# A written-out order of 1,900 steps: the same steps in another order

## The chip, the cores and the metric

The kernel runs on one core of a Trainium2 chip. The metric is the time of one execution in microseconds of device time, as the median of several runs.

## What is computed

A causal attention that lets every query see only its six best chunks of 32 keys, and a gated feed-forward network on its output. B, H, S, D are 4, 8, 768, 64; the network goes from 512 to 1536 and back, for 3072 tokens. The reference, cut:

```python
k_chunks = k.reshape(B, H, nc, chunk, D)
k_min, k_max = np.min(k_chunks, axis=3), np.max(k_chunks, axis=3)
ub = np.sum(np.maximum(q[:, :, :, None, :] * k_min[:, :, None, :, :],
                       q[:, :, :, None, :] * k_max[:, :, None, :, :]), axis=-1)
ub = np.where(causal, ub, -1000000000.0)
top_chunks = np.argsort(ub, axis=-1)[..., -top_k:]
scores = scale * np.matmul(q, k.transpose(0, 1, 3, 2))
scores = np.where(mask, scores, -1000000000.0)      # mask: chosen chunk and causal
attn = np.exp(scores - np.max(scores, axis=-1, keepdims=True))
attn = attn / (np.sum(attn, axis=-1, keepdims=True) + 1e-09)
...
x = np.ascontiguousarray(attn_out.transpose(0, 2, 1, 3)).reshape(B * S, H * D)
xn = x / np.sqrt(np.mean(x * x, axis=-1, keepdims=True) + 1e-06) * rms_g
g = xn @ w_gate
out = g * (1.0 / (1.0 + np.exp(-g))) * (xn @ w_val) @ w_out
```

## The kernel before, in words

**Tiles and stages.** The 32 heads go in 16 pairs, numbered 0 to 15; four pairs make one of the four batches. For each pair:

- `kload`, `qload` (line 500, on SP's queue; 192 KB each as two transfers of 96 KB) bring k and q; `v` (line 476, on POOL's queue) brings the values.
- `kT`, `qT` (line 520) turn three tiles of 128 at a time on TensorE; `kE`, `qE` (lines 290 and 294) copy the result out of PSUM, on ACT or on DVE.
- `kmx`, `kmn`, `dif` (lines 549, 551, 602) make the chunks' extremes; `relu` (lines 636 and 638, on ACT, DVE or POOL) the positive part of q; `ub` (lines 737 and 795) the bounds on TensorE; `ubE`, `up`, `ubm` bring them into place.
- `max`, `grd`, `sel` (lines 653 to 691) choose the chunks. The choice is laid beside k and q as further rows of the matrices `ke` and `qs`, so that a score of a chunk that is not chosen comes out very low. For the first three pairs it is turned on TensorE (`selT`, `selC`), later by a transposing transfer (`qX`, line 560). `kC`, `qC`, `qN` (line 294, mostly on POOL) cast k and q. The casts of a later pair write the same set of matrices (`set`, three of them) that an earlier pair's scores read.
- `sc` (line 882) computes scores of up to 512 columns, `exp` (line 899, on ACT) their exponentials, `mask` (line 905, on POOL) the causal edge, `av` (line 918) the products with v, `xb` (lines 938 and 939) the division.

A batch that is complete is normed in two halves (`sq`, `eps`, `root`, `xs`; then `tp` on TensorE and its eviction `tpE` for the first batch, a transposing transfer `xT` for the others). Each half of 384 tokens goes through the network: twelve times a `gate` (line 1051), `tanh`, `tg`, `val` (line 1072) and `hh`, then three output groups of three `po` steps each (line 1092), an eviction `poE` and a store `out`. The weights come in halves, wg and wv (line 440) and wo (line 445), from POOL's queue; the first six of the twelve gates read the first half of wg, the first six vals the first half of wv. `busy` (line 339) is a matmul of zeros, which keeps TensorE at work in the first microseconds.

So the network of one batch overlaps the attention of the next.

**The order.** Nothing decides at run time. Each step is added with its dependences to a list, and its place there is its number. A text, `PROGRAM`, names the steps in the order in which they are emitted: a letter for the engine (P TensorE, A ACT, D DVE, G POOL, S SP), the number, and behind the colon the slots of the buffers that the step opens (the eight PSUM banks among them). Each engine runs its words in order, and the order on each queue is that of the words as well:

```python
for word in program.split():
    n, _, slots = word[1:].partition(":")
    s = self.steps[int(n)]
    s.eng = engines[word[0]]
    new = [b for b in s.opens if b.slot is None]
    for b, x in zip(new, slots.split(",") if slots else (), strict=True):
        b.slot = int(x)
    out.append(s)
```

A step whose input is late holds back everything behind it on its engine. A buffer in the same slot must have been read by all its users before it is opened again.

Words that come up below: S227 is the load of pair 2's q, S541 of pair 6's k, S470 of pair 5's k; G115 and G183 load the v of pairs 0 and 1; G76 and G78 load the halves of wg, G77 and G79 those of wv; P1260, P1265 and so on in fives are the first gates, P1268 and P1288 two of the first vals; G415 and G486 are relus of pairs 4 and 5.

Of the kernel before, what the change touches and what calls it, by code (L numbers as in the profile page):

```python
# [28 lines left out]
    "S83:0 S88:1 S89 S82 D3 G0 D56 D55 D53 D54 D60 G63 A2 G65 P4:0 D59 P5:1 G66 P6:2 D58 P7:3 D57 G67 P8:4 S154:2 "  # L29
    "P9:5 G68 P86:6 S159:3 P10:7 G72 A87:0 P11:0 A69 D97:0 P92:1 D96:0 P12:2 G64 S335:4 G73 P84:3 D93:1 P90:4 A85 "  # L30
    "P13:5 P14:7 A91 P15:6 D95 P16:0 A99:0 P17:2 G101 D94 S222:5 P157:1 P155:5 D98 G62 A158:2 D103:3 P18:3 G61 "
    "P19:7 P20:4 S71 D156 P104:6,0 G102 D1 D52 D165:1 G168:1 P160:2 S330:6 A106:0 P162:3 D164:1 G74 A105 P21:1 "
    "A161:4 P107:7 A163 G167 P336:4 S70 D108:0 P338:5 A171:5 P22:0 G166 D109:2 P23:6 P24:1 A100 D110 S541:0 "
    "P172:2,3 A337:6 D112:0 A339 D111 P225:7 A173:0 D174 P113:0 G346:3 A226:1 S227:1 P175:6 A114 P223:1 D176:1 "
    "P25:4 P26:5 D177:3 P331:2 P333:3 D178 A224 G115:0 S404:2 P119:7 D332:2 A334 P147:6 A179:1 P135:4 D340:4 "
    "A148:0 G170 P128:5 P116:0 A136:1 D180 S399:3 P544:1 A117:2 D341:2 P150:3 P125:2 A545:0 P181:6 P141:4 A151:3 "
    "D232:5 A126:4 P138:0 G342 G236:2 P347:1,3 A120:5 D182 A129:6 G169 P228:2 A139:7 P230:7 S546:5 G183:1 D348:0 "
    "A349 P542:5 D229:5 A231 P350:6 D233:3 A142:8 P190:0 G345:0 P118:1 P121 A239:6 P144:3 P149:2 D351:2 P152 "
    "P184:7 G234 G235 A191:9 D352:6 P240:4,6 D543 A145:2 G238 D353 A185:5 P215:0 P122:5 G251:2 A241:0 D242 P143 "
    "A216:0 P146 P131:3 P243:7 A354 P405:4 A123:3 G237 D244:0 P209:6 P140 P137 A132:8 P218:0 D245:7 P193:7 A210:2 "  # L40
# [12 lines left out]
    "D423 A1281:1 D424 G1339:1 P1270:5 D1262:2 A1286:3 S426 D1282:4 P1275:2 A1271:5 D1346:3 P1263:3 A1276:6 S425 "
    "D1272:7 P1265:7 D1277:0 P1305:1 D1343:0 A1266:1 S559:0 P1288:5 D550 D1264:0 P1344:2 G557:3 P1315:0 D1287:5 "
    "A1345 S564:4 D1267:6 P439:3 A1316:2 P449:6 D1289:1 P445:2 P1300:7 A450:3 D1269:2 P1295:5 G427:0 A440:4 "
    "D481:2 A1301:3 P1283:6 A446:7 D1317:1 G79 A1296:5 P457:4 D1302:6 P560:3 A458:6 P436:2 G482 D1297:2 P1347:0 "
    "G81 A561:1 P562:7 D1348 P565:4 A563 D1284:3 P428:5 P463:3 A437:0 D1340:1 P432:0 G572:0 P487:7,6 A429:2 "
    "D570:3 A464:9 P1273:2 G451 A489:0 D488 A566:4 P1341:5 G485:0 P567:3 A1306:3 D1342 P459:6 A433:1 P490:7 "
    "D1274:4 G430 P1364:4 D569:2 G80 P466:5 P1349:0 A467:5 D491:0 P465 P442:2 D571 D568 P1399:5 A443:8 D1307:5 "
    "P460:7 P452 D575:2 A1400:4 P1278:3 A461:6 D1401:7 P577:2,1 A1350:3 D492:3 A1365:4 D493 G494 P453:7 P1308:5 "  # L60
    "A582:0 D578 A454:9 P1298:1 D1309:5 G455 P583:2 G484:2 D1299:6 P579:7 P462 D1366:5 P456 P1389:5 G434 D581:2 "
    "G483 D580:1 P468 P1392:1 D585 A1390:2 D584 D469:1 G573 P1310:4 D586:4 P1318:7 D592:5 D495 P1402:2 D1351:4 "
    "S496 P1374:6 D1279:7 D1391:3 P438:0 P1354:3 S497 D1393:8 P1303:5 D1403:9 A1355:0 P1367:1 A1375:2 D587 "
    "A1311:3 S700:3 D1319:10 P1290:2 G588 D1356:7 G498:1 P1379:7 D1312:1 A1291:0 P1293:3 D1368:11 A1380:3 G576:2 "
    "D1304:12 P524:4 P1325:1 D1292:5 A525:3 G574:0 D1294:13 P503:5 P444 D1381:6 P510:2 G526 P431 P447 P528:4 D593 "
    "A511:6 P1313:3 D589 A529:9 G594 P435 D1376:0 P703:7 S591 A504:5 P701:2 D1314:14 P1394:4 D595 D702:0 P537:6 "
    "P507:5 S590 P520:3 A538:0 D704 A1395:5 P1326 A521:8 D1396:3 P513:2 G522 S597 P1359:6 A514:2 P539:7 P441 "
    "P499:3 P1327 D448 A500:7 S596 A1360:2 P534:4 G501 P598:2 D1328:0 P1352:0 A535:1 G505 S682:1 A508:0 P516:3 "
    "P523 P506:1 D1353:15 P1384:4 A599:4 D1361:1 A517:8 P530 P536 P531:5 S705:5 D710:7 A1385:5 P512 P509 P665:0 "
    "A532:5 G714:2 P515 P678:2 P527 D1386:4 P672:3 A666:9 P518 P675:6 G558:3 D711:1 S841:2 P533 A673:1 P606:5 "  # L70
    "P502 P669:4 A679:6 P644:0 A676:0 D540 P661:3 G667 P1320:2 A607:2 G713 S823:0 D519 A662:3 P685:6 A670:8 "
    "P674:7 G663 P680 P623:5 D686:5 P657:3 P668 P683:1 G715:1 S687:6 A658:5 A645:7 P671 P1321 D684 A624:1 G646 "
    "D693:2 P648:4 G625 P651:6 S1329 P640:3 A649:6 P654:0 D692:0 P612:1 A641:9 P1322 A613:8 G642 P677 P706:5 "
    "D1323:1 G696:0 A655:0 P650:4 P842:3 S828:4 D707:3 A652:6 P647 P614:1 G712 P609:2 G600 P656 A843:4 P664 "
    "P626:0 P643 A610:7 P653 D681 G694 P633:5 S1324 P708:6 A634:8 P659 P615:3 P601 P826:2 A709 P611 P824:7 S846:3 "
    "D827:2 P602:5 G716:6 P630:6 A825 D660 P1369:2 A616:0 A603:3 D834:0 P1357:7 A631:1 S987:1 P608 A1370:2 P619:3 "
    "D833:6 P690:4 G604 A620:9 P636:5 P617 P635 G699:0 P688:6 D1371:5 A691:1 P605 P627:3 A689 P632 S982:5 D618 "
    "P844:2 G858:1 A628:6 P1362:4 D1358:16 A845 P629 A698:0 P831:6 D852:3 G621 P1382:1 A637:5 G854:1 P622 P638 "
    "P718:3,7 D639 G695 D1363:17 A1425:1,0 G697:0 P1377:2 A1426:1 D719:0 G717:2 P849:5 A1424:2 P720:0 D850:5 "
    "P1404:4 A1510:2,0 G835 D1378:18 P847:3 D721:0 A1405:2 P829:5 D832:1 A1511:1 P1330:2 D1427:3 D1406:7 G1428:4 "  # L80
    "A848 D722:1 P1407:6 A830 A723 D1429:2 P1387:4 D1433:0 P724:3 S1430:1 P1331 D1408:19 D1383:20 P1397:0 S1434 "
    "D1431:3 P1372:5 D1398:21 P1409:7 S1432 D1388:22 D1373:23 P1419:6 D726 S1105:0 D733:5 P1414:1 D734 D725 P1420 "
    "G735 D736 P1415 D851:7 S737 P1455:0 D727:0 D728 P1440:4 S738 A1456:1 D730 P1332 A729 D853 A839:0 S731 "
    "P1460:5 A1441:0 A1512:2 P1410 A1461:2 S732 A1333:2 P1445:3 D1462:7 D1442:6 P983:2 P1411 D1513:6 S969:2 "
    "A984:3 G1514:1 A1446:3 P789:5 P785:4 D1412:0 G856:1 P1421 A790:4 S1334 D1447:4 A786:7 G838:0 S1413 P792:2 "
    "D857:6 P760:7 A1422:1 P781:5 S1110:6 G855 P747:3 A793:2 P1450:4 D1457:5 A748:0 D1517:1 P753:6 A782:8 P1470:2 "
    "S964:3 A761:3 P739:0 D1519:2 P1435:3 A1471:2 G762 A740:1 D1472:0 P1108:5 S1123:4 A1436:3 P743:7 G783 P1438:0 "
    "D1109:4 A1451:1 D1437:2 A754:6 P1416 S1520 A744:9 P755:2 P1106:5 G745 D1417:2 P816:3 G741 P746 S1128:0 "
    "P795:6 D1452:3 A817:5 P791:7 P1443:1 G840:3 D1439:24 A1107 P742 P819:4 P750:3 D1444:25 S1423 P1465:0 A820:6 "
    "G787 A796:9 D1115:3 S1518 P859:5,4 A751:4 A1466:1 D1515:0 S1418 D1467:2 P967:1 S1516 A864:0 D860 P756:6 "  # L90
# [1073 lines left out]
```

## Time and profile before

| | |
|---|---|
| Time, median of 3 runs | 313.3 us (311.66 to 313.52) |
| Time of the profiled execution | 312.63 us |
| Its span, first to last instruction | 310.9 us |
| TensorE busy | 300.8 us (97%) |
| VectorE (DVE), ScalarE (ACT), GpSimd (POOL) busy | 232.2, 182.2, 119.5 us |
| Granted TensorE clock | 0.999 |
| Read from and written to memory | 28.57 and 6.29 MB |

The profile is one execution. Its page gives busy times of the engines, a row of 40 slices for each, the chain of work that ended last, and groups of instructions by line; further views give every instruction in order of time, the waits, busy times by stretch, and a transfer's time from issue to landing. The ends of matmuls are modelled, so a busy TensorE is not one at its peak. A profile's "[0.51 <-DMA qnat]" says that the engine was idle for 0.51 us before this row and what ended it.

### The profile page before, as it was taken

The page shows a single profiled execution, that of the slowest core. Times are in us where ns is not written, and L with a number is a line of the kernel's source. Part 1 is how long each engine was busy: PE and PEld are TensorE (multiplying, and loading weights), DVE is VectorE, ACT ScalarE, POOL GpSimd, SP SyncE. Part 2 cuts the span into 40 slices and gives each one's busy share as a digit, 9 for nine tenths or more (in the row PEclk, how much of TensorE's full clock was granted, in tenths as well). Part 3 has the DMA queues.
Part 4 walks back from the last instruction along what each step waited for, and adds up shares of the span by engine and source line. Part 5 has one row for each costly group of instructions (what it writes and reads, how often), then busy time and mean ns, then how long its engine had stood idle before and what let it go on. Part 6 is the DMA issues. An engine that isn't in the chain of part 4 may idle for free.

```text
span 310.9 us, 7415 instructions
## 1 busy us (share of the span) xinstructions
PE 300.8 (97%) x2764; PEld 190.4 (61%) x2782; DVE 232.2 (75%) x651; ACT 182.2 (59%) x405; POOL 119.5 (38%) x176
## 2 busy tenths in 40 slices
PE   7989998999999999999999999999999999999995
PEld 3657875666667764667776456666665455565542
DVE  5888988998977887789987897875743764477621
ACT  5789987672588763866997336667872303433110
POOL 8588856654547840632775104514030110000000
PEclk9999999999999999999999999999999999999999
DMA  9999999999999997996237136533000055200013
GB/s 172 221 170 175 121 209 209 158 168 150 154 176 206 201 163 145 231 163 165 55 26 50 33 74 178 53 74 29 3 0 2 34 86 186 102 2 0 0 70 136
DMA packets 113300, 35.35 MB, mean 114 GB/s; under 512 B 106224, under 2 KB 110064, under 8 KB 113264
## 3 DMA queue, kind: packets, MB, share of 16 engines
q1 hardware_dynamic: 83152, 26.62, 43.0%
q0 software_dynamic: 28512, 7.87, 25.4%
q10 hardware_dynamic: 1600, 0.39, 0.6%
q8 instruction: 22, 0.36, 0.5%
q14 instruction: 14, 0.11, 0.1%
HBM read 28.57 MB, written 6.29 MB: 112 GB/s over the span
## 4 chain that ended last, share of the span: by engine, by line
PE 87%; DMA 8%; POOL 2%; ACT 1%; issue 1%; ACTq 0%; SPq 0%; POOLq 0%
PE vp L1072 20%; PE po L1092 20%; PE gp L1051 19%; PE sc L882 10%; PE av L918 6%; DMA wg<-in_moe_w_gate_dram 5%; PE pq L520 3%; PE pk L520 3%; PE ub L795 2%; DMA knat<-in_k_dram 2%; PE ub L737 1%; DMA qnat<-in_q_dram 1%; POOL ke L294 1%; PE up L817 1%; PE busy L339 1%; POOL rt L638 1%
## 5 line engine op out<-in xcount | busy, mean ns | idle before, releaser
L899 ACT ACTIVATE pt<-sc 128x512 bf16<-128x512 f32 (+1 forms) x192 | 94.0, 556 | 21.2 <-PE sc L882 18.4
L1058 ACT ACTIVATE sg<-gp 128x384 bf16<-128x384 f32 x96 | 45.7, 495 | 72.2 <-PE gp L1051 62.6
L1072 PE MATMUL vp<-xT,wv 128*128 128x384 bf16 x384 | 74.4, 326 | 1.6 <-DMA wv<-in_moe_w_val_dram 1.5
L1051 PE MATMUL gp<-xT,wg 128*128 128x384 bf16 x384 | 74.2, 326 | 0.1
L1092 PE MATMUL po<-wo,hh 128*128 128x512 bf16 x271 | 66.8, 379 | 0.7
L1064 DVE SCALAR_TENSOR_TENSOR tg<-sg,gp 128x384 bf16<-128x384 bf16 x96 | 51.9, 549 | 20.6 <-ACT sg L1058 19.2
L1080 DVE TENSOR_TENSOR hh<-vp,tg 128x384 bf16<-128x384 f32 x96 | 51.5, 552 | 18.5 <-PE vp L1072 17.7
L882 PE MATMUL sc<-qs,ke 128*128 128x128 bf16 (+4 forms) x420 | 59.3, 251 | 0.0
L1072 PEld LDWEIGHTS <-wv 128*128 128x128 bf16 x384 | 35.8, 98 | 26.4 <-DMA wv<-in_moe_w_val_dram 1.8
L1051 PEld LDWEIGHTS <-wg 128*128 128x128 bf16 x384 | 35.7, 98 | 22.5 <-DMA wg<-in_moe_w_gate_dram 0.5
L1092 PEld LDWEIGHTS <-hh 128*128 128x128 bf16 x288 | 27.5, 98 | 27.5
L918 PEld LDWEIGHTS <-pt 128*128 128x128 bf16 x672 | 34.8, 98 | 11.1 <-POOL pt L905 0.3
L918 PE MATMUL av<-vx,pt 128*128 128x65 bf16 x672 | 41.2, 193 | 0.1
L905 POOL TENSOR_SCALAR_AFFINE_SELECT pt<-pt 128x512 bf16<-128x512 bf16 (+1 forms) x48 | 24.5, 522 | 38.5 <-ACT pt L899 38.1
L882 PEld LDWEIGHTS <-ke 89*128 89x128 bf16 (+1 forms) x420 | 31.0, 97 | 10.0 <-issue 1.4
L294 POOL CAST ke<-kt 64x768 bf16<-64x768 f32 x30 | 25.3, 846 | 7.3 <-PE sc L882 2.8
L987 POOL TENSOR_TENSOR ri<-ms,mhalf 128x3 f32<-128x3 f32 x8 | 7.2, 904 | 33.6 <-DVE ms L979 33.5
L995 DVE SCALAR_TENSOR_TENSOR xs<-xb,ri,gains 128x512 bf16<-128x512 bf16 x24 | 17.2, 751 | 3.1 <-POOL ri L987 2.9
L939 DVE TENSOR_TENSOR xb<-av,rden 128x384 bf16<-128x384 f32 (+1 forms) x34 | 18.2, 534 | 1.2
L520 PE MATMUL pk<-ident_f,knat 128*128 128x128 f32 x96 | 16.0, 282 | 1.7 <-DMA knat<-in_k_dram 1.7
L476 POOL DMA_DIRECT2D vx<-in_v_dram x16 | 17.3, 1079 | 0.1
L653 DVE MAX8 m<-ubm 128x8 f32<-128x8 f32 (+4 forms) x192 | 16.8, 160 | 0.2
(91 smaller groups left out, 300.6 us busy)
## 6 DMA issues: line engine op xcount, KB each, us to landing
out_dram<-osb SPq DMA_DIRECT2D x24, 256.0 KB, 2.3
knat<-in_k_dram SPq DMA_DIRECT2D x30, 192.0 KB, 4.4
qnat<-in_q_dram SPq DMA_DIRECT2D x30, 192.0 KB, 5.1
vx<-in_v_dram POOLq DMA_DIRECT2D x16, 192.0 KB, 5.9
wg<-in_moe_w_gate_dram POOLq DMA_DIRECT2D x2, 768.0 KB, 11.7
wv<-in_moe_w_val_dram POOLq DMA_DIRECT2D x2, 768.0 KB, 10.6
wo<-in_moe_w_out_dram POOLq DMA_DIRECT2D x2, 768.0 KB, 11.8
qs<-qn SPq DMA_TRANSPOSE x26, 2.8
```

The lines of the kernel that those rows point to most:

```text
L294: engine[e].tensor_copy(out_, in_)
L520: nc.tensor.transpose(t[:, j * P:(j + 1) * P], nat[w].tile[:, j0 + j].rearrange("p h d -> p (h d)"), ident_f[:])
L882: nc.tensor.matmul(t[:, x:x + m, :].rearrange("p a b -> p (a b)"), ke[kk, kb * P:(kb + 1) * P], qs[kk, q0 * P:(q0 + m) * P], start=not tri ...
L899: nc.scalar.activation(out=t[:, 0:nn, :], in_=sc.tile[:, 0:nn, :], func=ACT.Exp, scale=SCALE)
L905: nc.gpsimd.affine_select(out=pt.tile[:, 0:nd, :], in_=pt.tile[:, 0:nd, :], compare_op=ALU.is_ge, fill=0.0, base=0, pattern=[[0, nd], [1, ...
L918: nc.tensor.matmul(av.tile[:, qi - i0, :], pt.tile[:, x, :], VX[c.v.slot][:, hl * NT + kb, :], start=(begin and m == 0), stop=(left[0] == ...
L1051: nc.tensor.matmul(t[:], wg[:, g, hs], XT[b].tile[:, g, cols], start=(g == 0), stop=(g == NP - 1))
L1058: nc.scalar.activation(out=t[:], in_=gp.tile[:], func=ACT.Tanh, scale=0.5)
L1064: nc.vector.scalar_tensor_tensor(out=t[:], in0=sg.tile[:], scalar=1.0, in1=gp.tile[:], op0=ALU.add, op1=ALU.mult)
L1072: nc.tensor.matmul(t[:], wv[:, g, hs], XT[b].tile[:, g, cols], start=(g == 0), stop=(g == NP - 1))
L1080: nc.vector.tensor_tensor(out=t[:], in0=vp.tile[:], in1=tg.tile[:], op=ALU.mult)
L1092: nc.tensor.matmul(po.tile[:], hhs[ht].tile[:, th * P:(th + 1) * P], wo[:, ht, :], start=(ht == 0), stop=(ht == NHT - 1))
```

## The change

Only `PROGRAM` is another text. The steps, their dependences and the sizes of the pools are the same; one `busy` step (29) is left out, so that 25 of 26 stay. Steps that two or three engines may take have changed engines in places: 13 `qE` (9 from DVE to ACT, 4 the other way), 13 `kE` (5 and 8), 11 `ubE` (7 and 4), 11 `poE` (4 and 7), 10 `sq` (6 and 4), 5 `relu`, 12 `grd`, 8 `dif` (between DVE and POOL), 3 `tpE`, 2 `qN` (from POOL to DVE) and 2 casts. Nearly all lines of the text differ; these are the ones with the words above:

```diff
-    "A161:4 P107:7 A163 G167 P336:4 S70 D108:0 P338:5 A171:5 P22:0 G166 D109:2 P23:6 P24:1 A100 D110 S541:0 "
-    "P172:2,3 A337:6 D112:0 A339 D111 P225:7 A173:0 D174 P113:0 G346:3 A226:1 S227:1 P175:6 A114 P223:1 D176:1 "
-    "P25:4 P26:5 D177:3 P331:2 P333:3 D178 A224 G115:0 S404:2 P119:7 D332:2 A334 P147:6 A179:1 P135:4 D340:4 "
...
-    "A284:9 P273 P366:5 G76 D270 A363:8 P285 A360:3 P389:1 G77 P371:0 P364:6 P386:3 D329 A367:4 P361 P373:2 "
-    "A390:6 G411 D365 G553 P368 P395:4 G78 A387:0 P471:5 D372 P416:7,1 D472:6 A1248:2,0 D1246:1 A1247:2 P379:6 "
...
-    "P1260:7 A1336:5,0 D421:7 G413 P1280:1 A1335:1 D480:6 P1268:4 A1337:2 G414:0 D422 A1261:0 P1285:6 D1338:0 "
...
-    "D481:2 A1301:3 P1283:6 A446:7 D1317:1 G79 A1296:5 P457:4 D1302:6 P560:3 A458:6 P436:2 G482 D1297:2 P1347:0 "
...
+    "D108:0 P338:5 A171:5 G170:1 P21:6 D109:2 S71 P22:0 P23:7 A69 G166 D110 G345:0 P172:1,2 S227:0 D112:0 G169 "
+    "P24:4 P25:3 A111 D173:0 P26:6 A174 D339:6 P113:0 A101 G102 P175:7 S541:1 P225:4 A114 G115:0 D176:1 P336:3 "
...
+    "A337 P116:6 A231:5 P119:3 A229 D342 D346:4 A142:4 P212:0 P215:2 D233:3 A213:5 P347:5,4 S470:4 A126:6 D232:5 "
...
+    "P263 G76 P366:7 A287:1 A363:7 D270 P288 P276 A360:8 P392:5 G77 P273 P473:3 A367:5 D550:3 P371:6 P376:4 "
+    "A393:6 P361:2 D329 G78 P382:7 P364 P471:1 A377:0 P368 D365 P389:5 G411 A383:4 P395:0 G556:0 D372 A472:5 "
...
+    "D385 P28:1 P1275:0 D480:5 A1336:6,0 P1285:3 A1337:2 D421:7 P1270:5 A1335:1 D422 P1280:4 A1286:0 D423 D1338:0 "
+    "D424 A1271:1 G1339:2 P1265:1 D1287:2 A1276:3 S426 D1272:4 A548 P1288:3 A1281:5 D1346:3 G557:6 A561:4 P1278:2 "
+    "S425 A1266:6 D1277:7 P1347:5 P1263:7 D1267:0 D1279:0 P1260:0 S564:1 D1282:1 P1283:1 D1340:0 A1261:3 G79 "
...
+    "P449:2 P567:0 A1365:5 G486:5 D1297:7 P1354:3 A450:2 D1317:4 A464:3 P1268:6 A1355:6 P1318:2 A568 D1269:5 "
```

The first val stood behind two gates (P1260, P1280, then P1268) and now stands behind five (P1275, P1285, P1270, P1280, P1265, then P1288).

232 rows, old and new, of the table PROGRAM are left out of this document.

## The prediction

> **What bounds the kernel now.** I read the page's busy rows and slices first, then the busy time by stretch, then TensorE's timeline for its gaps, then what ends each gap.
>
> ```profile
> span 310.9 us, 7415 instructions
> PE 300.8 (97%) x2764; PEld 190.4 (61%) x2782; DVE 232.2 (75%) x651; ACT 182.2 (59%) x405; POOL 119.5 (38%) x176
> ...
> PE   7989998999999999999999999999999999999995
> ...
> DMA  9999999999999997996237136533000055200013
> ```
>
> TensorE is busy 97% of the span and stays so from slice 8 to the last, where the output drains. The DMA engines are busy 90% or more up to about 115 us. So TensorE's own work sets the time; an order can win or lose only by TensorE's gaps.
>
> ```profile
> 16.00:24.00 8.00, 6.50 (x77) 4.43 (x76) 6.70 (x21) 6.78 (x15) 6.49 (x8) 1.00 1.21 178
> 24.00:32.00 8.00, 8.00 (x126) 6.32 (x125) 6.93 (x35) 7.73 (x19) 6.64 (x9) 1.00 1.50 158
> 32.00:48.00 16.00, 15.49 (x254) 12.36 (x250) 14.66 (x35) 14.81 (x36) 10.17 (x13) 1.00 1.22 172
> 48.00:64.00 16.00, 14.47 (x124) 9.06 (x124) 14.39 (x40) 11.70 (x28) 10.68 (x10) 1.00 1.19 171
> ...
> 208.00:224.00 16.00, 16.00 (x163) 10.79 (x160) 10.35 (x23) 12.05 (x26) 4.28 (x7) 1.00 0.28 34
> ```
>
> (Columns: length, then busy time of PE, PEld, DVE, ACT, POOL.) The idle time lies before 64 us: 1.50 + 0.51 + 1.53 us in three stretches. From 16 to 48 us ACT is busy 29.3 of 32.0 us; in the late stretch nothing is near TensorE.
>
> ```profile
> 6.03 0.86 PE L520 MATMUL pq<-ident_f,qnat 128*128 128x128 f32 x3 [0.51 <-DMA qnat<-in_q_dram]
> ...
> 20.75 0.52 PE L520 MATMUL pk<-ident_f,knat 128*128 128x128 f32 x3 [1.28 <-DMA knat<-in_k_dram]
> ...
> 42.09 0.52 PE L520 MATMUL pk<-ident_f,knat 128*128 128x128 f32 x3 [0.42 <-DMA knat<-in_k_dram]
> ...
> 48.99 1.46 PE L1051 MATMUL gp<-xT,wg 128*128 128x384 bf16 x8
> 51.90 0.82 PE L1072 MATMUL vp<-xT,wv 128*128 128x384 bf16 x4 [1.45 <-DMA wv<-in_moe_w_val_dram]
> ...
> 307.13 0.60 ACT L292 ACTIVATE osb<-po 128x512 f32<-128x512 f32 x1 [7.33 <-PE po L1092]
> ```
>
> Every gap before the tail that is worth something ends with a load: the first q, the k of pair 6 (20.75), the k of pair 5 (42.09), and the first half of wv (51.90). Together 3.7 us.
>
> **The change part by part.** No instruction is added but for what moves between engines; one of the 26 zero matmuls is gone. To compare the orders I lay TensorE's own work end to end in each PROGRAM, so each word gets a "place": the TensorE work ahead of it. Start time minus place is the "lateness" that gaps have built up. Prices of the steps are from the chain of waits (start, us, what):
>
> ```profile
> 7.77 1.08 PE busy L339 x5
> 8.85 0.66 PE pk L520 x6
> 10.15 1.01 PE ub L737 x24
> ...
> 25.96 0.23 PE sc L882 x4
> ...
> 56.04 0.82 PE gp L1051 x4
> ...
> 58.89 1.30 PE gp L1051 x8
> ...
> 69.31 1.45 PE ub L795 x32
> ...
> 85.88 0.86 PE po L1092 x4
> ```
>
> So a transposing step of three is 0.33, a gate or val step 0.65, an output step 0.86; a zero matmul I count 0.27, between 0.22 here and the slower first ones. The whole axis is 296.2 us before and 295.9 after. In the order before, the first gate stands at 41.7 and starts at 48.99 (lateness 7.3), the first val at 43.0 and starts at 51.90 (8.9). The first gate that needs the second half of wg stands at 46.9 and starts at 56.04 (9.2). The axis ends at 296.2, and the last eviction, which waits for the last output step, starts at 307.1 (10.9). Behind 57 us, lateness thus grows by only 1.8 in 250 us.
>
> *Loads.* The k of pair 6 moves from place 15.5 to 19.3; the k of pair 5 is issued at 19.0 instead of 30.7, for a use at 34.2. Both waits go: -1.28 and -0.42. But the q of pair 2 is now used at 15.8 instead of 18.1, and in SP's queue it takes the seat that the k of pair 6 had. Before, this seat and the next one did so:
>
> ```profile
> 15.06 5.55 DMA knat<-in_k_dram
> ...
> 14.48 1.23 SPq L500 DMA_DIRECT2D knat<-in_k_dram  x2
> 15.81 4.76 SPq L500 DMA_DIRECT2D qnat<-in_q_dram  x4
> ...
> L500 SPq DMA_DIRECT2D qnat<-in_q_dram x2: 488/1582/2676, 15.8 to 16.3; - x2
> ...
> DMA to landing us min/median/max: 5.6/6.3/7.1
> ...
> L476 POOL DMA_DIRECT2D vx<-in_v_dram x1: 1268/1268/1268, 17.5 to 17.5; - x1
> ...
> vx<-in_v_dram POOLq DMA_DIRECT2D x16, 192.0 KB, 5.9
> ```
>
> The seat's second half went out at 15.06 and landed 5.55 later, at 20.6. The next load went out at 16.3 and took 7.1: POOL's v of pair 0 came 1.2 us behind it and shared the engines. In the order after, POOL has one relu of 2.1 less and one cast of 0.85 more ahead of that v, which so comes near 16.3, again 1.2 us behind the q. So q lands between 20.6 and 15.06 + 7.1 = 22.2. Before the k's gap, lateness was 20.75 - 1.28 - 15.5 = 4.0, and nearer 3.8, as a matmul's modelled end hides a little of the gap. With 3.8 TensorE comes to place 15.8 at 19.6: a wait of 1.0 to 2.6, and I take 1.8, the middle. The gap does not vanish; it changes its name. Pair 1's v has 4.9 us of TensorE work ahead of its use instead of 7.1, and a v load takes 5.9 in the median: a wait of up to 1.5. I take 0.3, since POOL's issue is no later than TensorE's lateness makes it.
>
> ```profile
> 33.05 3.35 POOL L294 CAST ke<-kt 64x768 bf16<-64x768 f32 x4 [1.06 <-PE sc L888]
> 36.49 2.14 POOL L638 TENSOR_SCALAR rt<-qt 128x768 f32<-128x768 f32 x1
> 38.57 0.82 POOL L294 CAST ke<-kt 64x768 bf16<-64x768 f32 x1
> 39.34 0.82 POOL L440 DMA_DIRECT2D wg<-in_moe_w_gate_dram  x1
> 40.17 0.75 POOL L440 DMA_DIRECT2D wv<-in_moe_w_val_dram  x1
> ...
> 60.20 0.76 POOL L440 DMA_DIRECT2D wv<-in_moe_w_val_dram  x1
> ...
> DMA to landing us min/median/max: 9.5/10.6/11.7
> ...
> DMA to landing us min/median/max: 8.7/11.7/14.7
> ```
>
> (The last lines are wv's and wg's own: the first half of wv, issued at 40.17, landed 11.7 later at 51.9; the second 9.5 after 60.20.) *Weights.* In the order after, POOL does three casts (the first waits for the last score of pair 1, place 27.6), the same relu of 2.14 and one cast ahead of wg; before, four casts, the relu and one. With a lateness of 6.0 there, that is 33.9 + 3 x 0.85 + 2.14 + 0.85 = 39.4, so wv goes out at 40.2 and lands at 51.9. The first val now stands behind five gates, not two, at 45.3. With a lateness of 7.2 TensorE comes at 52.5: the wait of 1.45 is gone, with 0.6 to spare. Its cover is the three gates, 1.95 us; without them it would wait 1.35. The second half of wv, however, is used sooner: 8.1 us of TensorE work after its issue, not 10.0. Issued near 55.6, it lands 8.7 (wg's least) to 9.5 later, at 64.3 to 65.1, and TensorE comes at 56.9 + 7.3 = 64.2: a new wait of 0.1 to 0.9. The relu of pair 5 stands on POOL only 1.9 ahead of its ub and takes 2.14; that wait, 0.3 to 0.8, falls into the same microsecond. I take 0.6 for both.
>
> *Engines.* Net, 5 q evictions and 3 of bounds change from DVE to ACT, 3 of k and 3 of outputs the other way. An eviction of 128x384 costs about the same on both:
>
> ```profile
> L290 ACT ACTIVATE qt<-pq 128x384 f32<-128x384 f32 x20 | 9.2, 492 | 0.3 <-PE pq L520 0.3
> L294 DVE COPY qt<-pq 128x384 f32<-128x384 f32 x12 | 6.6, 554 | 2.1 <-PE pq L520 2.0
> ```
>
> What matters is where. Between the places 14 and 42 ACT gets +3 q, +1 k, +2 bounds and +1 xT evictions, less one square sum and two guards: about +1.8 us, in the stage where it is already busy 29.3 of 32. From 16.0 to the first gate ACT then has 31.8 us to do. At the share of 24 to 32 us (7.73 of 8, 0.966) that takes 32.9 and the gate starts at 48.9: lateness 6.8.
>
> *Sum of lateness.* 3.8 at place 13; q of pair 2 +1.8; small waits to the first gate +1.3 (before: from 5.2 at place 15.5 to 7.3, less pair 5's 0.6 and 0.2 at the q); v +0.3: 7.2 at the first gate by TensorE, 6.8 by ACT. I take 7.2. With 0.6 it is 7.8 at place 62, where the order before has 9.2. From there to the end I take the same 1.8, and 0.3 for what I can't see: 9.9 against 10.9, and 0.3 less work. That is 1.3 us off the profiled execution's 312.6: **311.3 us**, 0.6% under the median of 313.3 (311.66 to 313.52) and within what a measurement of this kernel can tell from no change (1%, 3.1 us).
>
> The tail is the same in both orders: three evictions around the last output step, and the final store behind them on SP.
>
> **The rivals.**
> *More is won.* The q lands at 20.6 (0.8 less), the second wv and the relu come in time (0.6 less), and the late stretch needs no reserve (0.3): 309.6. For it: from 24 to 32 us ACT ran at 0.966 without holding TensorE. Against it: the v behind the q, and the 1.9 us between relu and ub.
>
> *The waits only move.* The q lands at 22.2 (+0.8) and pair 1's v costs its full 1.5 (+1.2): 313.3. For it: both are POOL transfers that meet SP's, and that seat has taken 7.1 once. The Trainium skill ("DMA: Bandwidth & Descriptors", Queues, rings and completion order) says that each DMA engine goes round between the queues that have work, packet by packet; by that rule a v on POOL slows the q on SP however early the q was issued, and this is the likelier of the two ends. The 7.1 beside the 5.55 agrees with it.
>
> *Slower.* ACT becomes the bound of the early stage. If it reaches only the share of 16 to 24 us, 6.78 of 8 or 0.85, its 31.8 us take 37.4, and the first gate starts at 53.4, lateness 11.3. The exps come late, so the last scores, so POOL's casts into the same set, so wg and wv: nothing overlaps it away. The end moves 1:1: 311.3 + 4.1 = 315.4. It decides from a lateness of 8.5 at the gate, a share of 0.92; at 0.83 it is over 1% slower. For it: both ACT and DVE stand at 0.92 there; against: some of ACT's idle time was TensorE waiting for loads.
>
> **How the numbers follow.** Forecast 0.40, more is won 0.15, waits only move 0.17, ACT bound 0.22; 0.06 for a stall in the late 240 us that I haven't found, 318 or so. The forecast's own range is 309.8 to 313.0, from its bounds: q 1.0 to 2.6, v 0 to 1.5, wv and relu 0 to 0.9. Faster by over 1% (under 310.2): most of "more is won" and a little of the forecast, 0.19. Slower by over 1% (over 316.4): some two thirds of "ACT bound", as few points of share lie between 0.85 and 0.83, and the late stall, 0.21. Within 1%: 0.60. The range goes from 309.0, just under "more is won", to 317.0, past "ACT bound".
>
> **What would show it.** Right: no wait for knat at 20 us but one of 1 to 2.6 for the qnat of pair 2; no wait of vp for wv near 52 us; the first gate at 48.8 to 50, the first val at 52 to 53.3; a short wait near 64 us for wv or for rt on POOL; ACT busy over 30.5 of the 32 us from 16 to 48; TensorE at 15.9 of 16 in every stretch from 80 to 288 us. Wrong: a first gate after 51, which is the ACT rival; a gap of over 1 us behind 70 us, which no step here has; or a wv wait that is still there, which would say that the POOL queue and not the place of the val decides.

## The result, and the profile after

The changed kernel takes 316.41 us in the median of five executions (315.15 to 317.74), the kernel before 313.35 beside it (311.66 to 314.03): ratio of the means 1.011, interval 1.007 to 1.015. Timed again with the experiments: 317.43 (315.27 to 319.12) against 312.56, ratio 1.015, interval 1.009 to 1.021. The change makes this kernel 1 to 1.5% slower. The forecast was 311.3. One execution, of 1107.03 us, is left out of these numbers: in its profile TensorE was busy for 1100.3 us over the same 2781 matmuls and slow from the first of them on (the first six zero matmuls took 4.91 us, 2.74 in the kernel before), while the busy times of the other engines stayed within 8% of those below; it came once in ten, and its cause is open.

The profile below is of an execution of 319.12 us, 6.5 us over the 312.6 us of the profiled one before. It is the slowest of the nine; by the medians the change costs 3.1 to 4.9 us. Its page:

```profile
span 317.4 us, 7412 instructions
...
PE 303.4 (96%) x2781; PEld 190.9 (60%) x2781; DVE 230.8 (73%) x649; ACT 184.5 (58%) x416; POOL 114.5 (36%) x167
...
PE   8989898859999999999999999999999999999995
...
PEclk9999999979999999999999999999999999999999
DMA  9999999998799996978914493522000064100024
```

Slice 9 (63 to 71 us) has TensorE at half and, new, a granted clock under 0.8. By stretch (columns as before: length, busy time of PE, PEld, DVE, ACT, POOL, then the granted clock):

```profile
16.00:24.00 8.00, 7.15 (x83) 5.07 (x82) 7.58 (x24) 7.54 (x17) 4.22 (x6) 1.00 1.25 189
24.00:32.00 8.00, 7.96 (x124) 6.47 (x121) 5.77 (x33) 7.56 (x18) 6.87 (x10) 1.00 1.49 186
32.00:48.00 16.00, 14.14 (x227) 10.91 (x224) 12.72 (x31) 14.98 (x37) 10.91 (x13) 1.00 1.71 168
48.00:64.00 16.00, 13.57 (x114) 8.94 (x114) 14.69 (x42) 11.18 (x28) 9.94 (x10) 1.00 1.00 163
64.00:80.00 16.00, 12.61 (x121) 7.53 (x122) 8.46 (x27) 6.57 (x15) 4.95 (x7) 0.89 1.17 145
80.00:96.00 16.00, 15.74 (x155) 10.68 (x153) 12.42 (x51) 10.57 (x24) 6.84 (x11) 1.00 0.93 146
96.00:112.00 16.00, 16.00 (x201) 12.27 (x199) 14.62 (x26) 14.62 (x35) 10.63 (x17) 1.00 1.32 215
```

Before, the idle time of TensorE in these stretches was 1.50 + 0.51 + 1.53 + 0.16 = 3.7 us, only the last 0.16 of it behind 64. Now it is 0.85 + 0.04 + 1.86 + 2.43 + 3.39 + 0.26 = 8.8. The slower clock adds 1.4, as worked out below: 5.1 + 1.4 = 6.5, which is what is to be explained. So the whole loss lies before 96 us. TensorE's timeline names the gaps:

```profile
20.35 0.85 PE L520 MATMUL pq<-ident_f,qnat 128*128 128x128 f32 x6 [0.74 <-DMA qnat<-in_q_dram]
...
39.80 0.38 PE L882 MATMUL sc<-qs,ke 89*128 89x128 bf16 x4 [1.39 <-DVE kmx L549]
...
48.71 0.40 PE L1017 MATMUL tp<-ident_b,xs 128*128 128x128 bf16 x4 [0.90 <-DVE xs L995]
...
51.20 3.41 PE L1051 MATMUL gp<-xT,wg 128*128 128x384 bf16 x20
54.45 1.46 PE L1072 MATMUL vp<-xT,wv 128*128 128x384 bf16 x8
...
67.39 0.87 PE L520 MATMUL pq<-ident_f,qnat 128*128 128x128 f32 x3 [5.11 <-DMA qnat<-in_q_dram]
68.06 1.49 PE L1051 MATMUL gp<-xT,wg 128*128 128x384 bf16 x4
```

No wait for a k and none for wv are left, as forecast. But 5.1 us are lost at 62.3 us to one load, the q of pair 7 (word S564, used by P565). Before, there was no gap at P565. And 0.9 us at 48.7 wait for xs, which needs the gains (S75). The chain of waits carries both loads:

```profile
39.50 8.29 DMA gains<-in_moe_rms_g_dram
...
57.63 0.58 SPq L500
58.22 0.04 issue
58.26 8.99 DMA qnat<-in_q_dram
```

Both went out about 1 us later than before (the gains at 39.50 instead of 38.36, the first half of q at 57.63 instead of 56.80), but they took 8 to 9 us to land instead of 4. POOL's own timeline shows what goes out beside them:

```profile
39.10 0.82 POOL L440 DMA_DIRECT2D wg<-in_moe_w_gate_dram  x1
...
57.39 0.85 POOL L440 DMA_DIRECT2D wv<-in_moe_w_val_dram  x1
```

Before, wg went out at 39.34, 1.0 us behind the gains, and the second half of wv at 60.20, 2.8 us behind the last of q. Now wg is 0.4 us ahead of the gains, and wv 0.24 us ahead of the first half of q.

The late gains belong to this execution more than to the order. Four more profiles below have the same words up to there (the two runs with zero matmuls and the two that move only the second half of wv). In them the gains' issue ended 0.8 to 1.1 us ahead of wg's, they landed 3.8 to 5.0 us after it, and the first gate started at 48.7 to 49.6 instead of 51.2.

The price of the clock is read from a finer table of the same execution:

```profile
64.00:68.00 4.00, 0.61 (x3) 0.64 (x4) 0.00 (x0) 0.00 (x0) 1.27 (x1) 0.85 1.79 163
68.00:70.00 2.00, 2.00 (x11) 1.18 (x9) 1.70 (x3) 0.00 (x0) 0.00 (x0) 0.50 1.59 196
70.00:72.00 2.00, 2.00 (x17) 1.45 (x16) 0.64 (x2) 1.52 (x4) 0.00 (x0) 0.94 1.23 206
```

At 0.50 stand 1.2 + 2.0 + 0.24 = 3.4 us, of which 0.6 still belong to the gap; 2.8 us of work at half speed lose 1.4. The gate step at 68.06 took 1.28 to the next start instead of 0.65.

### The profile page after: what moved, and what is told of

Read it like the earlier page. It is cut to its first block, busy times and chain, and to the rows that moved or that the text cites. A ratio compares the mean times of both kernels' runs of the same rounds, so it can differ in the third digit from the quotient of the medians.

```text
span 1105.3 us, 7412 instructions
## 1 busy us (share of the span) xinstructions
PE 1100.3 (100%) x2781; PEld 474.5 (43%) x2781; DVE 237.2 (21%) x649; ACT 197.8 (18%) x416; POOL 113.5 (10%) x167
## 4 chain that ended last, share of the span: by engine, by line
PE 100%; ACT 0%; DVE 0%; issue 0%; ACTq 0%
PE po L1092 21%; PE gp L1051 21%; PE vp L1072 21%; PE sc L882 12%; PE av L918 6%; PE pq L520 4%; PE pk L520 4%; PE ub L795 2%; PE busy L339 2%; PE ub L737 2%; PE up L817 1%; PE sc L888 1%; PE up L761 1%; PE tp L1017 0%; PE st L708 0%; ACT osb L292 0%
## 5 line engine op out<-in xcount | busy, mean ns | idle before, releaser
L1072 PE MATMUL vp<-xT,wv 128*128 128x384 bf16 x384 | 256.4, 890 | 0.0
L1051 PE MATMUL gp<-xT,wg 128*128 128x384 bf16 x384 | 256.3, 895 | 0.0
L1092 PE MATMUL po<-wo,hh 128*128 128x512 bf16 x288 | 246.1, 1107 | 0.0
L882 PE MATMUL sc<-qs,ke 89*128 89x128 bf16 (+5 forms) x420 | 172.7, 603 | 0.0
L1051 PEld LDWEIGHTS <-wg 128*128 128x128 bf16 x384 | 82.5, 219 | 133.3 <-issue 132.3
L1072 PEld LDWEIGHTS <-wv 128*128 128x128 bf16 x384 | 80.4, 213 | 134.5 <-issue 133.5
L918 PEld LDWEIGHTS <-pt 128*128 128x128 bf16 x672 | 94.6, 187 | 59.4 <-issue 55.5
L1064 DVE SCALAR_TENSOR_TENSOR tg<-sg,gp 128x384 bf16<-128x384 bf16 x96 | 52.3, 550 | 271.1 <-ACT sg L1058 270.7
L882 PEld LDWEIGHTS <-ke 89*128 89x128 bf16 (+1 forms) x420 | 78.3, 207 | 67.1 <-issue 61.7
L918 PE MATMUL av<-vx,pt 128*128 128x65 bf16 x672 | 104.5, 353 | 0.0
L1080 DVE TENSOR_TENSOR hh<-vp,tg 128x384 bf16<-128x384 f32 x96 | 51.9, 554 | 223.2 <-PE vp L1072 223.0
L520 PE MATMUL pq<-ident_f,qnat 128*128 128x128 f32 x96 | 46.8, 697 | 0.0
```

Of the source, the lines that this page charges most:

```text
L520: nc.tensor.transpose(t[:, j * P:(j + 1) * P], nat[w].tile[:, j0 + j].rearrange("p h d -> p (h d)"), ident_f[:])
L882: nc.tensor.matmul(t[:, x:x + m, :].rearrange("p a b -> p (a b)"), ke[kk, kb * P:(kb + 1) * P], qs[kk, q0 * P:(q0 + m) * P], start=not tri ...
L918: nc.tensor.matmul(av.tile[:, qi - i0, :], pt.tile[:, x, :], VX[c.v.slot][:, hl * NT + kb, :], start=(begin and m == 0), stop=(left[0] == ...
L1051: nc.tensor.matmul(t[:], wg[:, g, hs], XT[b].tile[:, g, cols], start=(g == 0), stop=(g == NP - 1))
L1064: nc.vector.scalar_tensor_tensor(out=t[:], in0=sg.tile[:], scalar=1.0, in1=gp.tile[:], op0=ALU.add, op1=ALU.mult)
L1072: nc.tensor.matmul(t[:], wv[:, g, hs], XT[b].tile[:, g, cols], start=(g == 0), stop=(g == NP - 1))
```

## The experiments

The changed kernel once more, beside the kernel before, for the profile above:

> The changed kernel as it is, for a profile with TensorE at its full rate (the one at hand shows it at about a quarter of it from the first matmul on). Measured so far 315.2 to 317.7 us in five runs against 311.7 to 314.0 before. Theory A (early stage, ACT or loads): the first gate starts after 51 us and TensorE has no gap over 1 us behind 70 us. Theory B (late stretch): the first gate starts near 49.5 us and 2 to 4 us are lost behind 70 us. Theory C (clock): the granted clock is 0.993 to 0.995 in its runs against 0.999; the loss of 3 us is mostly matmuls that run slower in some stretch, with no gap before them.

317.43 us. No gap over 0.3 us lies behind 96 us, so neither the late stretch nor a slow clock of its own is the cause; the clock drops once, behind the gap. The mean granted clock lies between 0.989 and 0.995 in all nine executions of the changed kernel, so each very likely had such a drop (before, the profiled execution has 0.999). What was open was why the load is late, and three runs took that apart.

**Pair 7's q ahead on SP.** (SP's words alone.)

```diff
- S559:0 S75 S426 S425 S564:1
+ S559:0 S75 S564:1 S426 S425
```

> The changed order with one word moved on SP: S564, the load of pair 7's q, stands ahead of S426 and S425 (the transposes of pair 4's q, which wait for VectorE) instead of behind them. Nothing else is changed. Theory A (the load of pair 7's q is late because the second half of wv, 1.57 MB, and pair 7's v are given to the same DMA engines just ahead of it): the load goes out at about 40.5 us in place of 57.6, lands before 52, the gap of 5.1 us at TensorE's word P565 is gone and with it the drop of the clock behind it; 311 to 313 us, against 317.4 of the changed kernel. Theory B (SP's order alone makes it late): the same time, since the move heals both. Theory C (the loss lies in the late stretch, behind 96 us): 316 to 318.

(The 1.57 MB in this text and in the next is what half of wv reads from memory: 512 x 768 numbers of 4 bytes. The profile's 768 KB count what lands, as bf16. Its 192 KB are one half of a pair's k or q; the whole has 384 KB, and not the 192 KB that the section on the kernel gives.) 312.85 us (312.33 to 316.22), ratio to before 0.999, interval 0.996 to 1.002. The wait is gone and nearly all of the loss with it; that much both theories said. What it did not say: the q now stands at wg's side, and the weights land later. TensorE's timeline of this run:

```profile
49.78 3.42 PE L1051 MATMUL gp<-xT,wg 128*128 128x384 bf16 x20 [1.39 <-DMA wg<-in_moe_w_gate_dram]
54.31 1.48 PE L1072 MATMUL vp<-xT,wv 128*128 128x384 bf16 x8 [1.11 <-DMA wv<-in_moe_w_val_dram]
```

**The second half of wv behind both v's, on POOL alone.**

```diff
- G79 G482 G576:0 G483:0 G427:1 G80
+ G482 G576:0 G483:0 G427:1 G79 G80
```

> The changed order with one word moved on POOL: G79, the second half of wv, stands behind G427 (pair 4's v) instead of ahead of pair 7's v. SP's order is untouched, so the load of pair 7's q still goes out at about 57.6 us. Theory A: it shares the DMA engines with 0.39 MB of v in place of 1.57 MB of wv, lands at 61.5 to 63 and the gap at P565 shrinks from 5.1 us to under 1; the second half of wv lands at about 69 and its first use then waits 0 to 3 us: 312 to 315 us. Theory B (only SP's order matters): the gap stays, 316.5 to 319 us.

314.85 us (313.04 to 316.47), ratio 1.005, interval 1.001 to 1.008. SP's order is untouched, yet q lands 3.6 and 3.8 us after its issue. Theory B falls. wv itself is now late:

```profile
67.58 1.46 PE L1072 MATMUL vp<-xT,wv 128*128 128x384 bf16 x4 [3.14 <-DMA wv<-in_moe_w_val_dram]
```

**The same mistake put into the kernel before,** with one POOL word:

```diff
- G557:3 G427:0 G79
+ G79 G557:3 G427:0
```

> The order before the change with one word moved on POOL: G79, the second half of wv, stands ahead of G557 (relu of pair 6), so that it goes out at about 53.5 us, ahead of the loads of pair 7's k and q (55.6 and 56.8 us). Theory A: these two land 4 to 8 us later than before, TensorE waits 3 to 6 us for them at about 61 us and its clock drops behind the gap: 316 to 320 us, the loss of the change made with one word. Theory B: nothing in SP's order is changed, so 312 to 314 us as before.

325.42 us (324.70 to 327.46), ratio 1.040, interval 1.036 to 1.045: the loss is made, at twice the size expected, and not by the load alone. wv went out at 52.33, and beside it stood not only k and q of pair 7 but the transposes of pair 4's q (51.77 and 53.03). SP's issue of that k and q took until 64.59 (57.95 in the kernel before), and the second half of q landed at 73.97, 10.0 us after its issue. TensorE's timeline and its table by stretch:

```profile
52.05 0.91 PE L1072 MATMUL vp<-xT,wv 128*128 128x384 bf16 x4 [1.98 <-DMA wv<-in_moe_w_val_dram]
...
64.67 1.14 PE L882 MATMUL sc<-qs,ke 89*128 89x512 bf16 x6 [4.69 <-DMA qs<-qn]
...
74.10 0.87 PE L520 MATMUL pq<-ident_f,qnat 128*128 128x128 f32 x3 [3.03 <-DMA qnat<-in_q_dram]
```

```profile
52.00:56.00 4.00, 3.94 (x15) 1.97 (x16) 1.22 (x3) 0.93 (x2) 1.16 (x2) 0.58 1.36 157
56.00:60.00 4.00, 3.98 (x27) 2.29 (x25) 3.49 (x7) 1.63 (x4) 1.15 (x1) 0.99 1.29 77
60.00:64.00 4.00, 0.00 (x0) 0.00 (x0) 2.39 (x5) 0.49 (x1) 3.09 (x4) 0.86 1.26 176
64.00:68.00 4.00, 3.33 (x14) 1.92 (x15) 0.29 (x1) 1.74 (x4) 0.00 (x0) 0.50 1.66 195
```

One late transfer delays the next user, and the clock drops three times, once at each of these gaps: from 64 to 68 us TensorE worked at half speed, and again from 73 to 80.

**Filling the gap,** to price the clock: 23 zero matmuls straight ahead of P565, then 11.

```diff
+ P29:0 P30:0 P31:0 ... P51:0
  P565:0
```

> The changed order with 23 zero matmuls of 512 columns added on TensorE straight ahead of P565, the matmuls that wait for pair 7's q: some 5 us of work that fills the gap and does nothing else. It tells the wait itself from the drop of the clock behind it (granted clock 0.50 from 68 to 70 us). Theory A with the clock as a part of the price: the granted clock stays at 1.00 there and the time is 1 to 1.6 us below the changed kernel's, 315.8 to 316.5 us. If the drop of the clock costs nothing: the same as the changed kernel, 317 to 318. If most runs wait less than 5 us there, the matmuls themselves cost: 318 to 319.

> As with the 23 zero matmuls ahead of P565, but 11. With 23, each took 0.433 us (one after the other into one bank), 9.9 us in all, twice the wait that they were to fill; there the q of pair 7 landed at 65.1, 4.7 us after TensorE's last work. 11 of them take 4.8 us. If the drop of the clock behind the gap is a part of the price: granted clock 1.00 throughout and 1 to 1.6 us below the changed kernel's 317.4, so 315.6 to 316.5. If the drop costs nothing: 317 to 318.

With 23, 322.15 us (320.23 to 323.57): they took 9.9 us in place of 5, so this run says nothing of the clock's price, only that the clock stayed at 1.00. With 11, 315.02 us (314.98 to 315.42), ratio 1.006 to before, interval 1.004 to 1.009; that is 0.5 to 0.9% under the changed kernel's ratios. The clock holds:

```profile
59.63 4.70 PE L340 MATMUL busy<-zeros 128*128 128x512 bf16 x11
64.38 0.55 PE L521 MATMUL pq<-ident_f,qnat 128*128 128x128 f32 x3
```

The pq step is back at 0.38 from start to start (0.67 with the slow clock). So the drop is a real part of the loss, 1.4 us by the trace above. The difference of times, 1.4 to 2.8, can't price it: in this execution q landed at 62.41, 2.8 us after TensorE's last work, and the zero matmuls outlasted that wait by 1.9.

**The gains too.** S75 ahead of S475, with and without S564 ahead:

```diff
- S475:6 S559:0 S75
+ S75 S475:6 S559:0
```

> The changed order with two words moved on SP: S564 (pair 7's q) ahead of S426 as in the run that moved it alone (312.85 us), and S75 (the gains) ahead of S475 (pair 5's q). The gains' load lands before 41 us in place of 44 to 48. Theory F (loads land in the order in which they are given out, whichever queue gives them): in the run with q7 ahead the first gates waited for wg, which landed behind the first half of q7; moving the gains changes nothing of that, 312.3 to 313.2 us. Rival (the gains' load, which held tp1258 by 1.07 us in the changed kernel, still sets the first gates): 311.3 to 312.

> The changed order with one word moved on SP: S75 (the gains) ahead of S475 (pair 5's q), pair 7's q left behind the transposes. It completes the square of the two moves (none 317.4, q7 alone 312.85, both 310.76). Theory F (loads land roughly in the order of issue across queues): the gains land before 40 us, the wait of 1.07 us at tp1258 goes, and the wait at P565 stays at 4 to 5 us, since wv is still given out with or ahead of q7: 315.5 to 317. Rival (the early waits are made up again while TensorE waits for q7, whose load goes out when VectorE's selection is done and not by TensorE's place): the same as the changed kernel, 317 to 318.

Both: 310.76 us (309.81 to 312.22), ratio to before 0.994, interval 0.992 to 0.996, better than either expectation and the only version here that beats both kernels. The first gates no longer wait and wv hardly does:

```profile
48.31 3.41 PE L1051 MATMUL gp<-xT,wg 128*128 128x384 bf16 x20
52.17 1.47 PE L1072 MATMUL vp<-xT,wv 128*128 128x384 bf16 x8 [0.45 <-DMA wv<-in_moe_w_val_dram]
```

The gains alone: anything from 310.49 to 318.60, median 315.46, ten executions of one program. Its profiled one, of 318.6 us, shows a wait that neither theory had, for the second half of pair 7's k (SP's row, then TensorE's):

```profile
35.38 4.26 SPq L500 DMA_DIRECT2D knat<-in_k_dram  x2
```

```profile
50.64 0.88 PE L520 MATMUL pk<-ident_f,knat 128*128 128x128 f32 x3 [4.92 <-issue]
```

(The releaser is not resolved there; k's second half landed at 50.55.) SP's issue of that load ended at 39.64, POOL's of wg at 39.56. The order of the two hangs on a tenth of a microsecond. In the four executions of 310.49 to 314.55 us the mean granted clock is 0.998 to 1.000, in the six from 315.05 us on 0.988 to 0.994; so those six very likely had a gap that cost the clock. That it was this one was seen in one trace only.

**q behind the first weights, and all three moves.** S564 takes slot 4, which pair 5's k leaves, so it can't go out before 42 us; then also S75 ahead and S470 (pair 5's k) behind S356.

> As the run that moved S564 ahead of S426, but S564 takes the buffer that pair 5's k leaves (slot 4, and later words that took 1 and 4 are swapped), so that its load can't go out before about 43 us: after the first half of wg, the first half of wv and the second half of wg (39 to 41 us), and still ahead of the second half of wv (55 us). Theory F (loads land in the order of their issue, across queues): the weights land some 2 us earlier than with q7 at 38.6 us (49.73, 54.27 and 58.88 there), q7 lands just behind the second half of wg, and the waits of 1.4, 1.1 and 0.25 us at the first gate, first val and next gate mostly go: 309.5 to 311.3 us. Rival (the queues share the engines evenly, so q7 lands before the weights and holds them up as before): 312 to 313.

> The order with pair 7's q behind the weights, and two more words moved on SP: S75 (the gains) ahead of S475, and S470 (pair 5's k, which landed 12 us before its use) from ahead of S546 to behind S356, so that pair 6's q, pairs 1 to 3's v and the transposes of pair 3's q land some 1 to 2 us earlier. Theory F: the wait of 0.3 to 1.5 us at sc359 and av214, and that for the gains, go as well: 308.5 to 310.5 us. If these waits only move (to the weights, since the bytes ahead of them are the same): as the run without these two, 309.5 to 311.3. If pair 5's k now lands late (before, in the order before the change, it waited 0.42 us): up to 1 us above that.

Both misses. The first: 315.61 us (314.94 to 317.40), ratio 1.010, interval 1.007 to 1.013. The weights did land earlier, and the first gate and val cost little; but q, behind wg, landed at 58.26, and the transposes that follow on SP landed 7.4 and 7.7 us after their issue:

```profile
62.36 0.23 PE L882 MATMUL sc<-qs,ke 89*128 89x128 bf16 x1 [2.97 <-DMA qs<-qn]
```

I had priced the load and not what stands behind it. The second: 319.69 us (318.80 to 320.73), ratio 1.021, interval 1.018 to 1.024. There the second half of pair 7's k fell behind wg, and TensorE waited for it:

```profile
52.19 0.87 PE L520 MATMUL pk<-ident_f,knat 128*128 128x128 f32 x3 [7.92 <-issue]
```

**Two tests of the order of issue, moving POOL's words alone.** First, in that last order, wg and the first wv 1.05 us later:

```diff
- G76 G77 G78 G411 G556:0
+ G411 G556:0 G76 G77 G78
```

> The order with all three moves, in which TensorE waited 7.9 us at 44.3 for the second half of pair 7's k (given out at 38.52, 0.10 us behind the first half of wg at 38.42; landed at 52.10, while the first half of k7, given out at 37.63, landed at 42.62), with the three words G76, G77 and G78 on POOL moved behind G411 and G556, 1.05 us of work: the weights go out 1.1 us later, at 39.5 us, and so behind both halves of k7. SP's order is not touched. Theory F: the second half of k7 lands at 43.5, the wait of 7.9 us and the drop of the clock behind it go; what stays is the wait for the transposes of pair 4's q that q7 behind the weights makes (2.97 us in the run with that move alone): 311 to 314 us, against 319.7. Rival (k7 waits for something else, SP's queue or its own buffer): 318.5 to 320.5 us.

315.55 us (314.78 to 318.26), 4.1 us less (by the two ratios 3.4), with SP's order the same. k's second half landed 6.4 us after its issue instead of 13.6. SP's landings in the two runs, the order with all three moves first:

```profile
DMA to landing us min/median/max: 5.0/5.9/13.6
```

```profile
DMA to landing us min/median/max: 5.1/5.5/6.4
```

It missed the 311 to 314 expected: what is left is the wait for the transposes (2.35 us), 1.10 for the later wv and 0.75 at the k itself. Second, the changed kernel with the second half of wv 1.3 us later:

```diff
- G79 G482 G576:0 G483:0
+ G482 G576:0 G79 G483:0
```

> The changed order with one word moved on POOL by 1.3 us: G79, the second half of wv, stands behind G482 and G576 (0.25 and 1.07 us) instead of ahead of them. SP's order is untouched. In the runs so far, each load of SP whose issue ended at least 0.2 us before that of a half of wg or wv (768 KB each) landed within 2.5 to 6.4 us of its issue's end, and each that ended 0.05 us before it or later landed 6.8 to 16.6 us after. Theory F, in that sharper form: both halves of pair 7's q (issue ends 58.21 and 58.80 in the changed kernel) now end before wv's (58.24 there, about 59.5 here), land by 62.5, and the wait of 5.1 us at P565 falls under 1 us with the drop of the clock behind it; the second half of wv lands at 66 to 67.5, and its first use waits at most 1 us: 311 to 313.5 us, against 317.4. Rival (wv must be further off, as when it was put behind both v's, 314.85 with a wait of 3.1 us for wv; or the order in which the issues end means nothing): 314.5 to 318.

312.19 us (310.23 to 313.54), ratio 0.997, interval 0.995 to 1.000: as expected, some 5 us back for one word. In all ten executions the mean granted clock is 0.997 or more. q landed 3.6 and 3.9 us after its issue; TensorE's rows:

```profile
60.30 0.50 PE L520 MATMUL pq<-ident_f,qnat 128*128 128x128 f32 x3
...
66.25 0.82 PE L1072 MATMUL vp<-xT,wv 128*128 128x384 bf16 x4 [1.85 <-DMA wv<-in_moe_w_val_dram]
```

No gap at P565, no drop of the clock; wv waits 1.85, not the 1 at most that I gave it.

Put side by side, from the timelines of SP and POOL (end of issue: start plus duration) and the landings:

| kernel | SP's load: end of issue | POOL's weight: end of issue | SP's against POOL's | load lands after its end |
|---|---|---|---|---|
| before | gains 39.18 | wg 40.16 | -0.98 | 3.4 |
| changed | gains 40.34 | wg 39.92 | +0.42 | 7.4 |
| changed | q7, first half 58.22 | wv 58.24 | -0.03 | 7.3 |
| 23 zero matmuls | q7, first half 56.06 | wv 56.58 | -0.52 | 2.9 |
| 23 zero matmuls | q7, second half 56.65 | wv 56.58 | +0.06 | 8.5 |
| q7 ahead | q7, first half 39.08 | wg 39.11 | -0.04 | 10.2 |
| q7 and gains ahead | q7, first half 39.10 | wg 39.33 | -0.22 | 3.7 |
| gains ahead | k7, second half 39.64 | wg 39.56 | +0.08 | 10.9 |
| all three | k7, second half 39.90 | wg 39.24 | +0.66 | 12.2 |
| weights behind k7 | k7, second half 40.67 | wg 41.00 | -0.33 | 5.0 |
| wv one us later | q7, second half 56.40 | wv 57.62 | -1.22 | 3.4 |

In this table a load whose issue ends 0.2 us or more ahead of a weight's lands in 2.9 to 5.0 us, and one that ends at the same time or later in 7.3 to 12.2. The border is not sharp. Two loads of the gains that are not in the table lie between: 0.51 us ahead of wg they took 5.5 (q7 ahead), 0.28 ahead 6.4 (the kernel before with wv ahead). The transposes follow this less neatly: one that ended 1.56 us behind wv landed 4.6 us later.

Why so little decides is read from the packets in which the DMA engines move the bytes. The profile counts them by queue: q0 is POOL's, q1 SP's; then packets, MB, share of the engines. The changed kernel from 60 to 64 us, where wv and pair 7's q are under way together:

```profile
q0 software_dynamic: 413, 0.63, 91.0%
q1 hardware_dynamic: 424, 0.11, 20.3%
```

The kernel before from 56 to 60 us, where SP's loads run alone:

```profile
q1 hardware_dynamic: 3760, 0.93, 111.8%
```

Beside wv the two queues take turns, one packet each. But a packet of wv holds 1.5 KB and one of q 0.26 KB, so q moves at an eighth of the rate that it has alone. By these rows 192 KB take some 7 us beside wv and 0.8 alone (an estimate). What a load has not moved when the weight's packets begin moves at the low rate until the weight is through. With q7 ahead, from 44 to 48 us, the counts are 446 and 460; in the profile of the gains alone, from 43 to 47, they are 452 and 450.

## Why the prediction was wrong, by its own steps

*Bound.* Right in the main: TensorE's gaps move the end, and with them the clock that drops behind a gap, which the prediction had not priced. Last evictions: 307.13 before, and after

```profile
313.67 0.60 ACT L292 ACTIVATE osb<-po 128x512 f32<-128x512 f32 x1 [6.36 <-PE po L1092]
```

which is 6.5 later, as are the times.

*Loads.* Both k waits went, and the wait changed its name to pair 2's q, as said; it landed at 20.22 and cost 0.74, under the 1.0 to 2.6 given. The 7.1 us behind the upper bound was misread: 2.68 of them were SP's own issue, and from the issue's end that load landed in 4.5 us, sooner than the two ahead of it (4.9 and 5.1). Pair 1's v, 0.3 foreseen, cost 0.28. **The step that failed is this one's list: it prices four loads, and neither pair 7's q nor the gains is among them.** Of the two it is pair 7's q that counts, as the gains were late in one profile of five with these words. Both stand in SP's order ahead of their use by about as much as before, and I took them as free. What I had not asked is what POOL puts out beside them. The step on the weights works out that POOL's second half of wv goes out near 55.6 instead of 60.2 and asks only when its own user waits. The terms missing from the sum, in the profiled execution: 5.1 at P565, 1.4 for the clock behind it, 0.9 at tp for the gains, and 1.4 at the scores of pair 3 (39.80). The row names kmx, but by the time it was the second transpose of pair 3's q: it landed at 39.66, 7.2 us after its issue. A v of POOL went out 0.2 us ahead of it; but so it did in the four profiles with the same words, where that transpose took 5.8 to 6.2. Why it took longer here was not tested. The first two terms, 6.5 us, are what the order itself can cost; the wait at P565 would be 2.8 us in the run with 11 zero matmuls and 4.7 in that with 23 (from TensorE's last work to the landing of q).

*Weights.* wv's wait went: it landed at 52.3 (51.9 said), the first val came at 54.45. The second half of wv was waited for nowhere, but only because TensorE stood still in its place; with q in time it cost 0 in one order and 1.85 in another, against the 0.1 to 0.9 given.

*Engines, and the rival that ACT becomes the bound.* The first gate came after 51, which the prediction had called the sign of this rival. The sign was a bad one: it came in one profile of five with these words. With two SP words moved and every step of ACT as in the changed kernel, the first gate starts at 48.31, 0.5 us ahead of the range given, while ACT is nearly full (the run with q7 and the gains ahead):

```profile
16.00:24.00 8.00, 7.85 (x88) 5.61 (x86) 7.81 (x24) 7.99 (x18) 4.22 (x6) 1.00 1.30 204
24.00:32.00 8.00, 7.93 (x122) 6.12 (x121) 5.92 (x34) 7.55 (x18) 7.65 (x11) 1.00 1.43 174
32.00:48.00 16.00, 15.78 (x259) 12.69 (x259) 15.22 (x36) 15.99 (x40) 10.44 (x12) 1.00 1.29 194
```

ACT is busy 31.5 of the 32 us from 16 to 48, over the 30.5 said, and TensorE 31.6. The share of 0.85 that the rival feared was ACT waiting, not its limit. (DVE, which the rival put at 0.92 beside ACT, was busy 28.3 of the 32 us, 0.88.)

*Sum.* Lateness was said to be 7.2 at the first gate; it was 51.20 - 42.1 = 9.1 in the profiled execution, 6.6 to 7.5 in the four others with these words, and 6.2 in the run just shown. Behind place 62, 2.1 was said; from 96 us on TensorE's stretches are full. Had the loads been in time, the sum would have come out: 310.76 and 312.19 in the two runs that mend it, around the 311.3. That it is so near is in part luck: in the run just shown the 1.8 taken for pair 2's q is hardly there (TensorE is busy 7.85 of the 8 us from 16 to 24). Luck too is that the measured 316.41 lies under the 317.0 at which the range ends: that end was set for an ACT that bounds, which did not happen. And the bounds given for the forecast's own range add up to 309.6 to 313.6, not to 309.8 to 313.0.

*Waits only move.* Nearest in kind: POOL's transfers meeting SP's. It was priced at +2.0, at two other places. The Trainium skill's rule that it drew on ("DMA: Bandwidth & Descriptors", Queues, rings and completion order: each engine goes round between queues, packet by packet) agrees with this trace: 413 packets against 424. Who takes it for an even share of the bytes is misled by the sizes of the packets: that estimate, q's first half and as much of wv, is 384 KB, 2.4 us at the 163 GB/s of 48 to 64 us. It landed 7.9 us after its issue, 0.05 us behind the whole 768 KB of wv. The prediction's "however early" is not so either: a load that has moved before the weight's packets begin is through. What failed is not the rule but that it was asked only of two v's and never of wv and pair 7's q.

## What to carry over

Price every load in the stretch by what any other queue gives out around it, above all a large one in large packets: a small load that falls beside 768 KB here landed 4 to 9 us later. When two queues' issues end within some tenths of a microsecond of each other, which is first can change between executions: the gains ended 0.42 us behind wg in one profile and 0.8 to 1.1 ahead in four with the same words. A margin of 1 us, got by moving one word, was worth 5 us. Ask also what waits next behind the load that you move; twice here the next transfer took the wait over.

## What the runs showed of the hardware

Short gaps can cost the clock. A gap of 1.98 us (52.05, the kernel before with wv ahead) was followed by 4 us at a mean of 0.58, one of 3.14 (67.58, wv behind both v's) by 0.50 from 68 to 70. One of 2.97 (62.36, q behind the weights) was followed by 1.00, and so were gaps of 1.4. All gaps of 4.7 us and more were followed by some 3.4 us or more at 0.50. The trace records the clock in stretches of 3.41 us or a multiple of it (66.84 to 70.25 at 0.50 in the changed kernel), and that tells the cases apart: the 1.98 us lay whole within one such stretch (49.25 to 52.66), while the 2.97, counted on in steps of 3.41, fell on a border at 60.93, with 1.54 us on one side and 1.43 on the other. The Trainium skill ("TensorE: Matmul & The Clock Gate", Part 1: The HAM clock gate) tells of an activity window of about 3.4 us that runs freely, so that the same gap may or may not fill one. The stretches agree with that; but the window need not be idle throughout, since 1.98 us of 3.41 were enough here.

Zero matmuls of 512 columns one after the other into one bank took 0.433 us each at a granted clock of 1.00; five into different banks (7.77 in the kernel before: banks 5, 7, 6, 0 and 2) took 0.22 each. Whether the bank is the reason was not tried.
